# Half of the first product's tiles by seven products over halves of d and of tokens, in blocks 4 to 10 of a retention and Mish feed-forward kernel

## The chip, the cores and the metric

One core of one Trainium2 chip. The metric is the device time of one execution in microseconds (us), the median of several runs. Times inside an execution come from one profiled execution, counted from the start of its span. The engines are TensorE (PE for its matmuls, PEld for its weight loads), VectorE (DVE), ScalarE (ACT), GpSimd (POOL) and SyncE (SP), which issues the DMAs. Each engine takes its instructions in the order in which the program wrote them.

## What is computed

```python
B, H, S, D = 4, 8, 768, 64
state = zeros(B, H, D, D)
for t in range(S):
    state = gamma[h] * state + outer(k[:, :, t], v[:, :, t])
    y[:, :, t] = q[:, :, t] @ state / sqrt(D)
x = y.transpose(0, 2, 1, 3).reshape(3072, 512)
h = x @ w_in                       # 512 x 2048
g = h * tanh(log1p(exp(h)))        # Mish
out = g @ w_out                    # 2048 x 512
```

Inputs and output are float32; the kernel multiplies in float16 and sums in float32.

## The kernel before, in words

**Blocks.** The 3072 tokens are 24 chunks of 128. Block 0 has four chunks, blocks 1 to 10 have two each (256 tokens). The retention is done in chunks: scores and a mask within a chunk, an outer product k v for the state, and the past state for the rest. It yields y in PSUM, which is copied to `xt`, the transposed float16 input of the feed-forward part (128 partitions, 4 parts of d_model, and room for 512 tokens, of which blocks 1 to 10 use the first 256). `w_in` lies in SBUF as eight tiles `wins[s][j]` (128 x 4 parts of d x 256 columns), and `w_out` as four tiles.

**First product.** `g1(blk, u)` (L567) makes two of the sixteen 128-wide tiles of h at a time: for each tile four matmuls (L576) over the four parts of d, with 128x128 weights and 256 tokens as the moving columns, into one PSUM bank; ACT's Mish (L584) turns the bank into `g` in float16. Eight calls make the first product of a block: 64 matmuls and eight Mish operations of 128x512.

**Second product.** `seven(blk, ...)` (L648) computes out = g @ w_out for the 256 tokens by seven products instead of eight, over halves of tokens, of d_ff and of the output's columns. It needs sums of halves of g (`gsums`, made on DVE by `sums_a`, L637 and L638, `sums_b`, L642, and `sums_c`, L646) and sums of halves of w_out (`tmats`, made once, L621 to L624). Each product is eight matmuls of 256 columns (L668). Partial results are copied to SBUF on ACT (`snap`, L674) and added on DVE (`done`, L682); the last one, `done(1, 0)`, is a plain copy (L680).

**What lies between.** In the middle of `seven(blk)` the hook `retain(blk + 1, later)` (L534) issues on PE the past part of y for block blk+1 and, from block 3 on, the scores and outer products of block blk+2 (`ready`, L421 and L428), then the present part (`present_of`, L509); ACT copies y into `xt` (L563). A tiny DVE copy `seen` (L548) orders them. Of what `ready` left in PSUM, `settle(blk)` (L486) makes three states on DVE (L463 or L465, L474, L465), `mask_two(blk)` (L495) masks the scores (L498), and `leave(blk)` (L504) makes the last state (L477, L478), except at the end of a batch. For blocks after 3 (those that are not `tight`, L926) the three are called after the first `g1` of the block ahead (`plan[0]`, L936).

**Queues.** POOL casts the inputs q, k, v of later chunks (L368, L371, L373). In `seven` of blocks 1 and 4 to 7 it begins after `sums_b`, and in those of blocks 2 and 3 after `sums_c`, by way of a tiny POOL copy of `gsums` (`cast_behind`, L920). From block 3 on two chunks are cast in a block, until none is left. SP's queue issues the loads, the stores of the block before, and the DMA that transposes q and k (L379).

**PSUM.** Eight banks: three for the tag "mm", one for "px", and two double banks for "at". `g1` uses "px" for its calls 2 and 5 and "mm" for the others. `seven` uses "px" for four of its products in turn, the last of which `done(1, 0)` reads; the banks are given out in turn, and a new tile waits until the readers of the bank's last tile are done.

Of the kernel before, what the change touches and what calls it, by code (L numbers as in the profile page):

```python
# [9 lines left out]
FP16 = mybir.dt.float16  # L10
FP32 = mybir.dt.float32
AF = mybir.ActivationFunctionType
ALU = mybir.AluOpType
# [3 lines left out]
def kernel(  # L17
# [9 lines left out]
    nc = tc.nc  # L27
    B, H, S, D = q.shape
    d_model, d_ff = moe_w_in.shape
    P = 128  # L30
    C = 128
# [3 lines left out]
    TB = 512  # L35
    CPB = TB // C
    BLOCKS = [4] + [2] * ((NCK - 4) // 2)
    first = [sum(BLOCKS[:i]) for i in range(len(BLOCKS))]
    NFB = d_ff // P
    NBP = d_model // P  # L40
# [3 lines left out]
    scale = float(1.0 / np.sqrt(D))  # L44
    inv_boost3 = float(1.0 / BOOST**3)
# [14 lines left out]
    cpool = ctx.enter_context(tc.tile_pool(name="rn_const", bufs=1))  # L60
# [7 lines left out]
    gp = ctx.enter_context(tc.tile_pool(name="rn_g", bufs=2))  # L68
    op = ctx.enter_context(tc.tile_pool(name="rn_o", bufs=5))
    mmps = ctx.enter_context(  # L70
        tc.tile_pool(name="rn_mmps", bufs=3, space=bass.MemoryType.PSUM))
    pxps = ctx.enter_context(
        tc.tile_pool(name="rn_pxps", bufs=1, space=bass.MemoryType.PSUM))
    atps = ctx.enter_context(
        tc.tile_pool(name="rn_atps", bufs=2, space=bass.MemoryType.PSUM))
# [44 lines left out]
    gtiles, tmats, gsums = {}, [], []  # L120
    ONE = 3
    nload, ncast = [0], [0]
    stores, weight_left = [], []

# [64 lines left out]
    def store_due(now):  # L191
        while stores and stores[0][0] <= now:
            _, dst, osb = stores.pop(0)
            nc.sync.dma_start(dst, osb)
# [291 lines left out]
    def settle(blk):  # L486
        a = first[blk]
        u = held[blk][1]
        for j in range(2):
            us[a + j] = u[:, :, j]  # L490
        mid_of(a)
        state_of(a)
        mid_of(a + 1)

    def mask_two(blk):  # L495
        at = held.pop(blk)[0]
        am = tpp.tile([P, 2, 2, HP, D], FP16, name="am")
        nc.vector.tensor_tensor(  # L498
            am.rearrange("p a j i c -> p (a j i) c"), at.rearrange("p a j i c -> p (a j i) c"),
            tri_half.rearrange("p r c -> p (r c)").unsqueeze(1).broadcast_to((P, 4 * HP, D)), op=ALU.mult)  # L500
        for j in range(2):
            ams[first[blk] + j] = am[:, :, j]

    def leave(blk):  # L504
        state_of(first[blk] + 1)
# [61 lines left out]
    def g1(blk, u):  # L567
        nt = BLOCKS[blk] * C
        per = TB // nt
        aside = u % 4 == 2 if blk == 0 else u in (2, 5)  # L570
        pool, tag = (pxps, "px") if aside else (mmps, "mm")
        h_ps = pool.tile([P, per, nt], FP32, name="h_ps", tag=tag)
        for j in range(per):
            s, f = divmod(u * per + j, FPS)
            for bp in range(NBP):
                nc.tensor.matmul(  # L576
                    h_ps[:, j], wins[s][f // 2][:, bp, f % 2 * P:(f % 2 + 1) * P], xts[blk][:, bp, :nt],
                    start=(bp == 0), stop=(bp == NBP - 1))
        room = NFB * TB // (2 * nt)
        at0, lies = divmod(u * per, room)  # L580
        if lies == 0:
            gtiles[blk, at0] = gp.tile([P, room, nt], FP16, name="g", tag="g", bufs=3)
        gt = gtiles[blk, at0][:, lies:lies + per]
        nc.scalar.activation(gt, h_ps, AF.Mish, scale=inv_boost3)  # L584
        for j in range(per):
            gts[blk, u * per + j] = gt[:, j]
# [47 lines left out]
    def sums_a(blk, half):  # L634
        n = NFB // 4
        (s1, s2, _, _), a11, _, a21, a22 = sum_views(blk, slice(half * n, (half + 1) * n))
        nc.vector.tensor_tensor(s1, a21, a22, op=ALU.add)  # L637
        nc.vector.tensor_tensor(s2, s1, a11, op=ALU.subtract)  # L638
# [5 lines left out]
    def sums_c(blk):  # L644
        (_, s2, _, s4), _, a12, _, _ = sum_views(blk)
        nc.vector.tensor_tensor(s4, a12, s2, op=ALU.subtract)  # L646

    def seven(blk, masks, hooks, last):  # L648
        n, hf = NFB // 2, d_model // 2
        px = pxps.tile([P, hf], FP32, name="o_ps", tag="px")  # L650
        pb = mmps.tile([P, hf], FP32, name="o_ps", tag="mm")
        osb = [op.tile([P, d_model], FP32, name="osb", tag="osb") for _ in range(2)]

        def a(i, j):
            return lambda f: gts[blk, j * n + f][:, i * P:(i + 1) * P]

        def b(i, j):
            return lambda f: wouts[(i * n + f) // FPS][:, f % FPS, j * hf:(j + 1) * hf]

        def s(i):  # L660
            return lambda f: gsums[blk % 2][:, i - 1, f]

        def t(i):
            return lambda f: tmats[(i - 1) // 2][:, (i - 1) % 2, f]

        def mm(o_ps, x, w, first=False):
            for f in range(n):
                nc.tensor.matmul(  # L668
                    o_ps, x(f), w(f), start=first and f == 0, stop=f == n - 1,
                    skip_group_check=True)  # L670

        def snap(o_ps):
            x = op.tile([P, hf], FP32, name="snap", tag="snap", bufs=3)
            nc.scalar.copy(x, o_ps)  # L674
            return x

        def done(i, j, o_ps, plus=None):
            dst = osb[i][:, j * hf:(j + 1) * hf]
            if plus is None:
                nc.vector.tensor_copy(dst, o_ps)  # L680
            else:
                nc.vector.tensor_tensor(dst, o_ps, plus, op=ALU.add)  # L682
            if last:
                nc.sync.dma_start(out_rows(blk, i)[:, j * hf:(j + 1) * hf], dst)

        mm(px, a(0, 0), b(0, 0), True)
        m1 = snap(px)
        mm(pb, a(0, 1), b(1, 0), True)
        done(0, 0, pb, m1)
        sums_b(blk)  # L690
        if blk == 1 or not tight(blk):
            cast_behind(blk, 2)
        for fn, *args in masks:
            fn(*args)
        pe = mmps.tile([P, hf], FP32, name="o_ps", tag="mm")
        if last:
            mm(px, s(2), t(2))
            u2 = snap(px)
        mm(pe, s(1), t(1), True)
        m5 = snap(pe)  # L700
        if not last:
            mm(px, s(2), t(2))
            u2 = snap(px)
        for fn, *args in hooks[0]:
            fn(*args)
        sums_c(blk)
        if blk > 1 and tight(blk):
            cast_behind(blk, 3)
        for fn, *args in hooks[1]:
            fn(*args)  # L710
        mm(px, s(3), t(3))
        done(1, 1, px, m5)
        for fn, *args in hooks[2]:
            fn(*args)
        mm(pe, s(4), b(1, 1))
        done(0, 1, pe, u2)
        mm(px, a(1, 1), t(4))
        done(1, 0, px)
        if not last:
            for i in range(2):  # L720
                stores.append((1 + i, out_rows(blk, i), osb[i]))
# [208 lines left out]
    def plan_of(blk):  # L930
        a = first[blk] + 4
        plan = {u: [] for u in (0, 1, 4, 5, 7)}
        if tight(blk):
            plan[5] = [(get_ready, blk + 1)]
        elif blk + 1 < len(BLOCKS):
            plan[0] = [(settle, blk + 1), (mask_two, blk + 1), (leave, blk + 1)]  # L936
        if blk == 1:
            plan[0] += [(turn_next, a)]
            plan[1] += [(load_to, a + 3)]
        elif blk < ONE:  # L940
            plan[1] += [(next_chunk, a)]
            plan[4] += [(load_to, a + 4)]
        return plan

    first_block()
    for blk in range(1, len(BLOCKS)):
        last = blk + 1 == len(BLOCKS)
        plan = plan_of(blk)
        for u in range(NFB // 2):
            store_due(u)  # L950
            g1(blk, u)
            if u in ((6, 7) if tight(blk) else (5, 7)):
                sums_a(blk, u // 7)
            for fn, *args in plan.get(u, ()):
                fn(*args)
            if weight_left:
                weight_left.pop(0)()
        hooks = [[], [], []]
        if not last:
            later = blk + 2 if ONE <= blk < len(BLOCKS) - 2 else None  # L960
            hooks = [[(retain, blk + 1, later, True)],
                     [(next_two, first[blk] + 6, tight(blk))] if blk >= ONE else
                     [(turn_next, first[blk] + 5), (load_to, first[blk] + 8)] if blk == 1 else
                     [(next_chunk, first[blk] + n) for n in (5, 6, 7)],
                     [(finish, blk + 1)] if later is None else []]
        if tight(blk):
            hooks[2].append((leave, blk + 1))
        seven(blk, [(mask_two, blk + 1)] if tight(blk) else [], hooks, last)
# [31 lines left out]
```

## Time and profile before

| | us |
|---|---|
| median of 3 runs (lowest to highest) | 201.49 (201.34 to 202.06) |
| profiled execution | 201.44 |
| its span, first to last instruction | 199.7 |
| first product of a block, blocks 4 to 10 | 6.99 |
| from one first product's start to the next, blocks 4 to 9 | 14.71, 14.71, 14.71, 14.52, 14.59, 14.31 |
| from block 10's first product to the start of the last DVE copy | 13.29 |
| VectorE busy in those stretches, blocks 4 to 9 | 9.09, 8.62, 7.84, 7.83, 7.82, 7.74 |
| ScalarE busy in them | 7.22, 7.23, 7.22, 7.22, 7.21, 6.62 |
| GpSimd busy in them | 8.43, 6.67, 6.67, 6.48, 2.35, 0.00 |

A line of a timeline gives the start of an instruction, its length, engine, line in the kernel, operation, out<-in with partitions x elements and type, how many were merged, and in brackets the idle time before it with what ended it. The chain of work that ended last is followed back from the last instruction; each of its lines gives a start, a length and what ran. A matmul's own length (0.27 us for 256 columns) contains its way through the array; in a row they start 0.109 us apart. The granted TensorE clock was 1.00 in all stretches.

### The profile page before, as it was taken

To read this page: it belongs to the slowest core of one execution; us is meant where nothing else is said; L and a number is where in the kernel's file an instruction comes from. 1 tells how busy PE (TensorE), PEld (TensorE's weight loads), DVE (VectorE), ACT (ScalarE), POOL (GpSimd) and SP (SyncE) were. 2 spreads that over 40 slices of the span, in tenths; PEclk is the share of its full clock that TensorE was granted. 3 is DMA by queue.
4 is the path that set the end of the run, shared out by engine and by line. 5 is a ranking of instruction groups with operands and counts; after the bars stand their busy time and mean duration, and the time that the engine had idled before them with its cause. 6 is when DMAs were issued, how large, how long until landed. Compare 5 with 4: busy or idle time off the path is not lost.

```text
span 199.7 us, 6553 instructions
## 1 busy us (share of the span) xinstructions
PE 192.4 (96%) x2871; PEld 155.1 (78%) x2871; DVE 111.6 (56%) x204; ACT 92.1 (46%) x166; POOL 74.8 (37%) x93
## 2 busy tenths in 40 slices
PE   7887999999999999999999999999999999999993
PEld 7765444445888888888888888888888888888882
DVE  0688444997359169266836745545753654455052
ACT  2376773242542542554454454454553553642640
POOL 6562000669807603942907508409409300000000
PEclk9999999999999999999999999999999999999999
DMA  5999999999999999999999999996932600201102
GB/s 180 300 316 356 390 382 343 316 254 214 239 232 250 188 214 271 127 215 211 258 155 300 194 232 202 199 225 126 206 121 40 175 3 11 98 3 54 56 26 79
DMA packets 83612, 38.74 MB, mean 194 GB/s; under 512 B 57728, under 2 KB 77696, under 8 KB 83584
## 3 DMA queue, kind: packets, MB, share of 16 engines
q1 hardware_dynamic: 83440, 38.28, 82.0%
q8 instruction: 22, 0.36, 0.8%
q10 hardware_dynamic: 144, 0.05, 0.2%
q14 instruction: 6, 0.05, 0.1%
HBM read 27.31 MB, written 6.29 MB: 168 GB/s over the span
## 4 chain that ended last, share of the span: by engine, by line
PE 69%; DMA 16%; SPq 7%; DVE 3%; POOL 2%; issue 1%; DVEq 0%; POOLq 0%
PE h_ps L576 33%; PE o_ps L668 31%; DMA wi<-in_moe_w_in_dram 5%; DMA wt<-in_moe_w_out_dram 5%; SPq L243 3%; PE y_ps L509 3%; DMA qf<-in_q_dram 3%; DMA qkt<-qk 3%; SPq L160 2%; PE at L421 2%; PE u_ps L428 1%; POOL qk L368 1%; POOL qk L371 1%; DVE win L177 1%; DVE wout L188 1%
## 5 line engine op out<-in xcount | busy, mean ns | idle before, releaser
L576 PE MATMUL h_ps<-xt,win 128*128 128x256 f16 (+1 forms) x704 | 86.0, 282 | 0.8 <-ACT xt L358 0.7
L576 PEld LDWEIGHTS <-win 128*128 128x128 f16 x704 | 68.5, 98 | 16.0 <-POOL win L177 0.9
L584 ACT ACTIVATE g<-h_ps 128x512 f16<-128x512 f32 x96 | 57.3, 597 | 48.3 <-PE h_ps L576 48.3
L668 PEld LDWEIGHTS <-gsum 128*128 128x128 f16 x320 | 30.1, 98 | 4.5 <-DVE gsum L646 0.7
L668 PE MATMUL o_ps<-tmat,gsum 128*128 128x256 f16 x240 | 29.4, 273 | 0.0
L668 PEld LDWEIGHTS <-g 128*128 128x128 f16 x240 | 23.5, 98 | 2.7
L637 DVE TENSOR_TENSOR gsum<-g 128x512 f16<-128x512 f16 x20 | 8.6, 429 | 28.4 <-ACT g L584 28.4
L674 ACT COPY snap<-o_ps 128x256 f32<-128x256 f32 x30 | 11.2, 372 | 21.5 <-PE o_ps L668 21.5
L368 POOL TENSOR_TENSOR qk<-qf,qvs 128x512 f16<-128x512 f32 x18 | 19.5, 1086 | 3.6 <-DMA qf<-in_q_dram 2.5
L373 POOL TENSOR_TENSOR v<-vf,qvs 128x512 f16<-128x512 f32 x18 | 20.7, 1148 | 0.0
L923 POOL COPY summed<-gsum 128x1 f16<-128x1 f16 x7 | 1.3, 187 | 51.7 <-DVE gsum L642 36.9
L371 POOL TENSOR_TENSOR qk<-kf,qvs 128x512 f16<-128x512 f32 x18 | 20.1, 1118 | 0.0
L682 DVE TENSOR_TENSOR osb<-o_ps,snap 128x256 f32<-128x256 f32 x30 | 12.7, 424 | 12.4 <-PE o_ps L668 7.4
L668 PE MATMUL o_ps<-wout,g 128*128 128x256 f16 x160 | 19.1, 273 | 0.0
L563 ACT CAST xt<-y_ps 128x512 f16<-128x512 f32 x15 | 10.2, 733 | 11.3 <-PE y_ps L509 11.3
L590 PE MATMUL o_ps<-wout,g 128*128 128x512 f16 x64 | 15.0, 380 | 0.0
L465 DVE TENSOR_TENSOR mid<-u_ps,sth 128x256 f16<-128x256 f32 x15 | 6.3, 422 | 10.1 <-PE u_ps L428 9.8
L498 DVE TENSOR_TENSOR am<-at,tri_half 128x1024 f16<-128x1024 f32 x9 | 10.9, 1216 | 0.0
L590 PEld LDWEIGHTS <-g 128*128 128x128 f16 x64 | 5.8, 97 | 6.6
L668 PE MATMUL o_ps<-wout,gsum 128*128 128x256 f16 x80 | 10.4, 274 | 0.0
L668 PE MATMUL o_ps<-tmat,g 128*128 128x256 f16 x80 | 10.4, 273 | 0.0
L392 PE MATMUL at<-ident 128*128 128x128 f16 (+1 forms) x79 | 8.0, 276 | 1.4 <-POOL ident L96 1.4
(77 smaller groups left out, 184.0 us busy)
## 6 DMA issues: line engine op xcount, KB each, us to landing
kf<-in_k_dram SPq DMA_DIRECT2D x24, 256.0 KB, 4.8
vf<-in_v_dram SPq DMA_DIRECT2D x24, 256.0 KB, 5.3
out_dram<-osb SPq DMA_DIRECT2D x22, 256.0 KB, 3.9
qf<-in_q_dram SPq DMA_DIRECT2D x20, 256.0 KB, 4.1
wt<-in_moe_w_out_dram SPq DMA_DIRECT2D x3, 1024.0 KB, 9.8
wi<-in_moe_w_in_dram SPq DMA_DIRECT2D x4, 512.0 KB, 8.5
wi<-in_moe_w_in_dram SPq DMA_DIRECT2D x2, 1024.0 KB, 10.6
qfirst<-in_q_dram SPq DMA_DIRECT2D x2, 512.0 KB, 4.6
```

What stands on the lines that cost most here:

```text
L368: nc.gpsimd.tensor_tensor(q16.rearrange("p (r h) d -> p h r d", r=2), qf, qs_two[:, heads].unsqueeze(3).broadcast_to((P, H // 2, 2, D)), o ...
L371: nc.gpsimd.tensor_tensor(k16, kf, boosts.unsqueeze(2).broadcast_to((P, H, D)), op=ALU.mult)
L373: nc.gpsimd.tensor_tensor(v16, vf, vs[g % 2].unsqueeze(2).broadcast_to((P, H, D)), op=ALU.mult)
L498: nc.vector.tensor_tensor(am.rearrange("p a j i c -> p (a j i) c"), at.rearrange("p a j i c -> p (a j i) c"), tri_half.rearrange("p r c -> ...
L563: nc.scalar.copy(dst[:, :, :, s], src)
L576: nc.tensor.matmul(h_ps[:, j], wins[s][f // 2][:, bp, f % 2 * P:(f % 2 + 1) * P], xts[blk][:, bp, :nt], start=(bp == 0), stop=(bp == NBP - 1))
L584: nc.scalar.activation(gt, h_ps, AF.Mish, scale=inv_boost3)
L590: nc.tensor.matmul(o_ps, gts[blk, fb][:, t * P:(t + 1) * P], wouts[s][:, f, cols], start=(fb == 0), stop=(fb == NFB - 1))
L637: nc.vector.tensor_tensor(s1, a21, a22, op=ALU.add)
L668: nc.tensor.matmul(o_ps, x(f), w(f), start=first and f == 0, stop=f == n - 1, skip_group_check=True)
L674: nc.scalar.copy(x, o_ps)
L682: nc.vector.tensor_tensor(dst, o_ps, plus, op=ALU.add)
```

## The change

In blocks 4 to 10 the eight calls of `g1` are replaced by `mixed_in(blk, last)`.

- Tiles 4 to 7 and 12 to 15 of h are made as before, two at a time (`plain`).
- Tiles 0 to 3 and 8 to 11 are made by seven products of halves: halves of d_model, of the 256 tokens, and the two groups of four tiles. Each product (`mm`) is four tiles times two parts of d, that is eight matmuls with 128x128 weights and 128 tokens as moving columns, into one bank of 128x512. Three intermediate results go to SBUF by ACT copies (`kept`: m1, m5, u2), three sums are made on DVE from PSUM and SBUF (`plus`: h11, h12, h22), and Mish reads those from SBUF; the fourth quarter is read from PSUM.
- The sums of halves of `w_in` (`in_sums`) are made once on DVE: four operations of 128x512 each in block 2 and in block 3, one behind each of the first `g1` calls.
- The sums of halves of x (`x_sums`) are four DVE operations of 128x256 each, into the unused columns of `xt`. They are issued in `seven(blk)` for block blk+1, between `done(0, 1)` and the last product with `done(1, 0)`, for blk 3 to 9.
- `settle`, `mask_two` and `leave` for the next block move: `settle` ahead of the first of the products, `mask_two` behind the second, `leave` behind the sixth, ahead of `sums_a` for the first half.
- The banks: pp, pf, pa and the second plain pair take "mm" in this order; pm and the third plain pair take "px", the last plain pair takes "at".

```diff
+    def in_sums(j):
+        t = cpool.tile([P, 4, 2, TB // 2], FP16, name=f"wsum_{j}")
+        wsums.append(t)
+        (a11, a12), (a21, a22) = [(x[:, :2], x[:, 2:]) for x in (wins[0][j], wins[2][j])]
+        sub = ALU.subtract
+        return [
+            lambda: nc.vector.tensor_tensor(t[:, 0], a21, a22, op=ALU.add),
+            lambda: nc.vector.tensor_tensor(t[:, 1], t[:, 0], a11, op=sub),
+            lambda: nc.vector.tensor_tensor(t[:, 2], a11, a21, op=sub),
+            lambda: nc.vector.tensor_tensor(t[:, 3], a12, t[:, 1], op=sub),
+        ]
+
+    def x_views(blk):
+        xt = xts[blk]
+        b = [[xt[:, 2 * i:2 * i + 2, j * C:(j + 1) * C] for j in range(2)] for i in range(2)]
+        t = [xt[:, i, 2 * C:].rearrange("p (k c) -> p k c", k=2) for i in range(4)]
+        return b, t
+
+    def x_sums(blk):
+        ((b11, b12), (b21, b22)), t = x_views(blk)
+        for to, a, b in ((t[0], b12, b11), (t[1], b22, t[0]), (t[2], b22, b12), (t[3], b21, t[1])):
+            nc.vector.tensor_tensor(to, a, b, op=ALU.subtract)
+
+    def mixed_in(blk, last):
...
+        def mm(o_ps, w, x, begin=False):
+            for f in range(n):
+                for k in range(2):
+                    nc.tensor.matmul(
+                        o_ps[:, f], w(f // 2, k)[:, f % 2 * P:(f % 2 + 1) * P], x[:, k],
+                        start=begin and f == 0 and k == 0, stop=k == 1, skip_group_check=True)
...
+        def mish(to, src):
+            nc.scalar.activation(to, src, AF.Mish, scale=inv_boost3)
...
+        def kept(o_ps):
+            m = op.tile([P, n, C], FP32, name="hsum", tag="hsum", bufs=6)
+            nc.scalar.copy(m, o_ps)
+            return m
+
+        def plus(x, y):
+            m = op.tile([P, n, C], FP32, name="hsum", tag="hsum", bufs=6)
+            nc.vector.tensor_tensor(m, x, y, op=ALU.add)
+            return m
+
+        pp = bank(mmps, "mm", True)
+        pf = bank(mmps, "mm")
+        pa = bank(mmps, "mm")
+        if not last:
+            settle(blk + 1)
+        mm(pa, a(0, 0), b[0][0], True)
+        m1 = kept(pa)
+        mm(pf, s(1), t[0], True)
+        m5 = kept(pf)
+        if not last:
+            mask_two(blk + 1)
+        plain(pp, n)()
+        pm = bank(pxps, "px")
+        mm(pm, a(0, 1), b[1][0], True)
+        h11 = plus(pm, m1)
+        mm(pa, s(2), t[1])
+        u2 = kept(pa)
+        mish(part(0, 0), h11)
+        mm(pf, s(4), b[1][1])
+        h12 = plus(pf, u2)
+        mish(part(0, 1), h12)
+        plain(bank(mmps, "mm", True), n + 2)()
+        mm(pa, s(3), t[2])
+        h22 = plus(pa, m5)
+        mish(part(1, 1), h22)
+        if not last:
+            leave(blk + 1)
+        sums_a(blk, 0)
+        plain(bank(pxps, "px", True), 3 * n)()
+        mm(pa, a(1, 1), t[3])
+        mish(part(1, 0), pa)
+        ph = atps.tile([P, 2, 2, 2 * C], FP32, name="h_ps", tag="at")[:, 0]
+        plain(ph, 3 * n + 2)()
+        sums_a(blk, 1)
 
     def seven(blk, masks, hooks, last):
...
         mm(pe, s(4), b(1, 1))
         done(0, 1, pe, u2)
+        if not last and blk >= ONE:
+            x_sums(blk + 1)
         mm(px, a(1, 1), t(4))
         done(1, 0, px)
...
-        elif blk + 1 < len(BLOCKS):
-            plan[0] = [(settle, blk + 1), (mask_two, blk + 1), (leave, blk + 1)]
...
+        if blk > ONE:
+            mixed_in(blk, last)
+        elif blk > 1:
+            weight_left.extend(in_sums(blk - 2))
         for u in range(NFB // 2):
             store_due(u)
+            if blk > ONE:
+                continue
             g1(blk, u)
```

More of the change, by code (lines that the diff above doesn't have):

```diff
@@ L122 @@
     nload, ncast = [0], [0]
-    stores, weight_left = [], []
+    stores, weight_left, wsums = [], [], []
     def room(g):
@@ new lines, in x_views, with a, s, part @@
+    def x_views(blk):
[8 more added lines that the diff above has]
+    def mixed_in(blk, last):
+        b, t = x_views(blk)
+        n = NFB // 4
+        gt = gtiles[blk, 0] = gp.tile([P, NFB, 2 * C], FP16, name="g", tag="g", bufs=3)
+        for f in range(NFB):
+            gts[blk, f] = gt[:, f]
+        def mm(o_ps, w, x, begin=False):
[4 more added lines that the diff above has]
+                        start=begin and f == 0 and k == 0, stop=k == 1, skip_group_check=True)
+        def a(i, j):
+            return lambda h, k: wins[2 * i][h][:, 2 * j + k]
+        def s(i):
+            return lambda h, k: wsums[h][:, i - 1, k]
+        def mish(to, src):
+            nc.scalar.activation(to, src, AF.Mish, scale=inv_boost3)
+        def part(i, j):
+            return gt[:, i * 2 * n:i * 2 * n + n, j * C:(j + 1) * C]
+        def plain(h_ps, f0):
+            for f in range(2):
+                w, h = divmod(f0 + f, n)
+                for k in range(NBP):
+                    nc.tensor.matmul(
+                        h_ps[:, f], wins[w][h // 2][:, k, h % 2 * P:(h % 2 + 1) * P],
+                        xts[blk][:, k, :2 * C], start=k == 0, stop=k == NBP - 1)
+            return lambda: mish(gt[:, f0:f0 + 2], h_ps)
+        def bank(pool, tag, whole=False):
+            return pool.tile([P, 2, 2 * C] if whole else [P, n, C], FP32, name="h_ps", tag=tag)
+        def kept(o_ps):
[40 more added lines that the diff above has]
+        sums_a(blk, 1)
```

## The prediction

> **What bounds the kernel now.** First the page's busy times, then the chain of work that ended last, then the timelines of VectorE (DVE) and GpSimd (POOL) where one block ends and the next begins.
>
> ```profile
> PE 192.4 (96%) x2871; PEld 155.1 (78%) x2871; DVE 111.6 (56%) x204; ACT 92.1 (46%) x166; POOL 74.8 (37%) x93
> ```
>
> TensorE (PE) is busy for 96% of the span. The chain, printed as start, length, what, says that in blocks 4 to 10 it is the bound by itself; one block's start:
>
> ```profile
> 110.57 6.99 PE h_ps L576 x64
> 117.56 3.49 PE o_ps L668 x32
> ```
>
> The first product's 64 matmuls take 6.99 us, 109 ns each, in every one of the seven blocks, with no wait in them; the period of a block is 14.71 us in blocks 4 to 6, then 14.52, 14.59 and 14.31. A PE saving would thus count in full, if nobody comes late. DVE at such a boundary (start, length, line; blocks 5 to 6, whose first product begins at 125.12, called T0 below):
>
> ```profile
> 124.52 0.42 DVE L682 TENSOR_TENSOR osb<-o_ps,snap 128x256 f32<-128x256 f32 x1 [0.59 <-PE o_ps L668]
> 125.32 0.42 DVE L680 COPY osb<-o_ps 128x256 f32<-128x256 f32 x1 [0.38 <-PE o_ps L668]
> 125.66 0.41 DVE L465 TENSOR_TENSOR mid<-u_ps,sth 128x256 f16<-128x256 f32 x1
> 126.11 0.42 DVE L474 TENSOR_TENSOR sth<-u_ps,mid 128x256 f16<-128x256 f32 x1
> 126.57 0.42 DVE L465 TENSOR_TENSOR mid<-u_ps,sth 128x256 f16<-128x256 f32 x1
> 126.91 1.21 DVE L498 TENSOR_TENSOR am<-at,tri_half 128x1024 f16<-128x1024 f32 x1
> ```
>
> DVE works through this without a gap, and nobody waits for it, since the next sums are due only at T0+6. POOL is casting in the same stretch:
>
> ```profile
> 121.71 1.04 POOL L371 TENSOR_TENSOR qk<-kf,qvs 128x512 f16<-128x512 f32 x1
> 122.71 1.49 POOL L373 TENSOR_TENSOR v<-vf,qvs 128x512 f16<-128x512 f32 x1
> 124.17 1.05 POOL L368 TENSOR_TENSOR qk<-qf,qvs 128x512 f16<-128x512 f32 x1
> 125.19 1.03 POOL L371 TENSOR_TENSOR qk<-kf,qvs 128x512 f16<-128x512 f32 x1
> 126.19 1.03 POOL L373 TENSOR_TENSOR v<-vf,qvs 128x512 f16<-128x512 f32 x1
> ```
>
> And DVE's sum s4, two f16 inputs in SBUF, beside them:
>
> ```profile
> 121.83 1.47 DVE L646 TENSOR_TENSOR gsum<-g,gsum 128x1024 f16<-128x1024 f16 x1
> ```
>
> Alone that shape takes 0.68 (L646 at 165.74). Here it ends at 123.30, so it worked from 122.62, 0.13 before the POOL record at 121.71 ends; and the next POOL operation took 1.49 for 1.04. The two engines exclude each other. Two such sums in a row lose to POOL each time:
>
> ```profile
> 35.70 1.55 DVE L621 TENSOR_TENSOR tmat<-wout 128x1024 f16<-128x1024 f16 x1
> 37.28 1.43 DVE L622 TENSOR_TENSOR tmat<-wout,tmat 128x1024 f16<-128x1024 f16 x1
> ```
>
> Sums that read PSUM (L465, L682) keep their 0.42 beside POOL.
>
> **The change, part by part.** *PE.* 32 matmuls of 256 columns (32 x 0.109 = 3.49 us) become 56 of 128 columns. No steady stretch of before has these in a first product; nearest are the transposes, 128 columns with new weights each:
>
> ```profile
> 6.21 0.62 PE L215 MATMUL t_ps<-ident,qk 128*128 128x128 f16 x8
> 6.21 0.45 PEld L215 LDWEIGHTS <-qk 128*128 128x128 f16 x8
> ```
>
> (0.62 - 0.22) / 7 = 57 ns, the 0.22 being one matmul's own length. The ends are 50 ns (the weight loads' spacing, (0.45 - 0.10) / 7) and 98 ns (a load's own length); I take 56.5. A product is then 0.45 us, seven 3.16, and the stage 6.65 against 6.99: 0.34 less per block, 2.4 us in seven blocks, if PE never waits.
>
> *Operations added, per block.* ACT copies m1, m5, u2 (128x512, PSUM): L219's 0.58; ends 0.37 (256 wide, L674) and 0.73 (L563). DVE adds h11, h12, h22 (128x512, PSUM plus SBUF): between 0.42 (256 wide, L682) and 1.22 (1024 wide, L498), on that line 0.69, and L602's copy of that size has 0.68; I take 0.69. DVE's x_sums, four of 128x256 f16: L637 (512 wide) 0.42 and L646 (1024) 0.68 give 0.295; ends 0.16 (the one-column copy) and 0.42; I take 0.30. Mish is as often and as wide as before; half of it reads SBUF (L256 there: 0.63 for 0.60). Back to back, ACT operations start 0.1 and DVE's 0.07 before the one ahead ends.
>
> *DVE's queue.* x_sums stands between L682 (ends T0-0.18) and L680, which frees the bank px; behind L680 wait settle (L465, L474, L465), mask_two (L498), and only then h11, h12, h22. POOL's L368 ends at T0+0.10, L371 and L373 follow at once. So t0 works from -0.03 to 0.27; L371 then ends at 1.17, t1 works 1.04 to 1.34; L373 ends at 2.24, t2 works 2.11 to 2.41; POOL is done, t3 ends at 2.64. The four, 1.1 us alone, take 2.8. L680 then starts at 2.57 and ends at 2.99; by the spacings above settle starts 0.34 later, mask_two another 1.25, h11 another 1.13: h11 from 5.29 to 5.98, h12 to 6.60, h22 to 7.22.
>
> *PE against it* (0.06 from a DVE end to PE). M1, M5 and the first plain pair end at 1.78. The next product needs px: 3.05, a wait of 1.27, with all of PE's later work queued behind it. It, two more products, a plain pair and another product end at 5.73. The plain pair in px needs h11: 6.04 (wait 0.31), ends 6.91. The last product needs h22's read: 7.28 (wait 0.37), and the last pair ends at 8.61. ACT starts the first mixed mish at 6.03 and has six in a row: the one that frees px ends at 8.72, so the second product starts at 8.78 instead of 6.99: **+1.79 per block**. ACT's last ends at 9.70; its values are used at about 10.4, and sums_a ends at 10.6 where the second product's first add on DVE is due at 10.8. So the rest keeps its length.
>
> *By blocks.* 5, 6, 7: 3 x 1.79 = 5.37. Block 8: POOL's L368 ends 0.25 later against T0 (154.70): 2.04. Block 4: four POOL operations (95.51 to 99.57) lie behind L682, and which engine is first at 95.5 is open: 1.6 to 3.4, I take 2.5. Blocks 9, 10: POOL is through at 156.7, x_sums ends by T0+0.9. In 9, h22 ends at 5.47 and PE and ACT lose 0.35 again: 0.0. Block 10 has no settle or mask: PE waits only 0.07, -0.27.
>
> *in_sums*, four sums of 0.42 in blocks 2 and 3: in block 2 DVE has been idle for 4.98 us before L465 (70.82), which hides them. In block 3 (idle 4.78) POOL casts from 80.08 to 87.34; the four end at about 85.4, just ahead of L465 at 85.84, but push POOL by some 1.2 us, and with it the transposing DMA issued at 86.58, whose 4.7 us to landing ended near the use at 92: 0 to 0.8, I take 0.4. No path below nothing: they free nothing.
>
> settle, mask_two and leave come later but their readers (past_of, ready) stand 10 us on. The stores keep their order in SP's queue; POOL's queue still starts from sums_b.
>
> Sum: 2.5 + 5.37 + 2.04 + 0.0 - 0.27 + 0.4 = **+10.0 us**. The profiled execution took 201.44 (span 199.7, 1.7 around it; the median of the runs is 201.49): **211.5 us**.
>
> **Rivals.** *A, DVE keeps the way free* and x_sums runs in 1.1 us beside POOL as well. For: t1 to t3 follow closely. Against: L622. Then blocks 4 to 8 go like 9: 0.0 each, so -0.27 + 0.4: 201.6, no change.
>
> *B, the PE saving comes through.* Place: DVE's queue before h22. It decides at L680 starting by T0+0.6 (h22 ends 4.65 after it, PE gets there at 5.3), with the mish in px done in time. Then -2.4 us: 199.0. For: block 10 nearly does it. Against: even without POOL, L680 starts at 0.8; with it, at 2.6.
>
> *C, weight loads pace the small matmuls.* At 98 ns a product takes 0.78 and the stage at least 7 x 0.78 + 3.49 = 8.98, so blocks 9 and 10 lose 2.0 each. In blocks 5 to 7 the third product still starts at 3.05, and what follows it (five products at 0.78, three pairs at 0.87) ends at 9.6 without a wait: +2.6 each; block 8 +2.85, block 4 +3.3, block 3 +0.4; in all +18.3: 219.8. For: PEld's 98 ns is longer than 57. Against: the transposes, eight in a row.
> The Trainium skill ("TensorE: Matmul & The Clock Gate", Back-to-back issue gap) puts a steady stream of load and matmul with 128 columns at about 81 ns each. By it a product would take 0.65 and the time come to about 214.8, my estimate from that page; the transposes here, at 57, don't show it, though they are only eight at a time.
>
> **Numbers.** Forecast 0.78, A 0.09, B 0.08, C 0.05. The forecast's own bounds: if t1 and t2 pass in one POOL gap, 0.9 less in each of five blocks, and block 3 and 4 at their low ends: 205.5; if x_sums' operations take 0.42 (+0.25 a block), ACT gives no overlap (+0.4 a block) and blocks 3 and 4 stand at their high ends: 217. The range 205.5 to 217 holds the forecast and C's lower half, about 8 in 10. A run of this kernel can tell about 0.5% (1.0 us) from no change: faster 0.08 (B), same 0.09 (A), slower 0.83.
>
> **What would show it.** x_sums' rows: with POOL busy, about 0.5 to 1.1 each in blocks 5 to 8, 0.30 in 9 and 10. PE idle before the third product of blocks 4 to 8 with DVE's L680 named. The first stage 8.6 us in blocks 5 to 7 and about 7 in block 9. Products at 0.45 us, else C. If the stage is 6.65 throughout, or x_sums rows are all 0.3, the forecast is wrong; also if the second product grows, for I cost it at nothing.

## The result, and the profile after

The changed kernel takes 211.25 us against 201.49: a ratio of 1.0474 (95% interval 1.0444 to 1.0503), slower. Of its four runs three took 210.95 to 211.44 us; the fourth, in a slow state, took 388.21 us, counts in the median and not in the ratio. The prediction was 211.5 us, range 205.5 to 217. The profiled execution took 211.44 us, 10.0 us more than that of before; its span is 209.5 us, 9.87 us more.

In the listing after the change L682 is a small product, L702 a plain pair, L669 x_sums, L717 the adds h11, h12, h22; old L668, L680 and L682 are now L775, L787 and L789, and old L584 stands as L693 in the mixed blocks. The busy times of the page:

```profile
PE 194.0 (93%) x3039; PEld 155.4 (74%) x3039; DVE 148.5 (71%) x261; ACT 100.4 (48%) x187; POOL 76.4 (36%) x93
```

TensorE's share of the span fell from 96 to 93%: it now waits. The chain of work that ended last, over the stage that before read "110.57 6.99 PE h_ps L576 x64" and nothing else (here block 6, first product from 130.13 to 138.79):

```profile
129.95 0.44 DVE xt L669
...
130.41 2.27 DVE xt L669 x3
132.68 0.35 DVE osb L787
...
133.07 1.07 PE h_ps L682 x16
...
134.18 0.45 DVE am L498
...
135.31 0.69 DVE hsum L717
...
136.03 2.73 ACT g L693 x5
```

It no longer lies on TensorE: it runs through x_sums, the copy that frees px, mask_two, the adds and the Mish operations behind them. The timelines of DVE, of POOL and then of PE in that stretch:

```profile
129.52 0.42 DVE L789 TENSOR_TENSOR osb<-o_ps,snap 128x256 f32<-128x256 f32 x1 [0.59 <-PE o_ps L775]
129.87 2.81 DVE L669 TENSOR_TENSOR xt<-xt 128x256 f16<-128x256 f16 x4
132.60 0.41 DVE L787 COPY osb<-o_ps 128x256 f32<-128x256 f32 x1
...
134.18 1.21 DVE L498 TENSOR_TENSOR am<-at,tri_half 128x1024 f16<-128x1024 f32 x1
135.31 1.88 DVE L717 TENSOR_TENSOR hsum<-h_ps,hsum 128x512 f32<-128x512 f32 x3
```

```profile
129.18 1.05 POOL L368 TENSOR_TENSOR qk<-qf,qvs 128x512 f16<-128x512 f32 x1
130.19 1.08 POOL L371 TENSOR_TENSOR qk<-kf,qvs 128x512 f16<-128x512 f32 x1
131.24 1.09 POOL L373 TENSOR_TENSOR v<-vf,qvs 128x512 f16<-128x512 f32 x1
```

```profile
130.13 0.61 PE L682 MATMUL h_ps<-xt,win 128*128 128x128 f16 x8
130.57 0.61 PE L682 MATMUL h_ps<-xt,wsum 128*128 128x128 f16 x8
131.02 1.04 PE L702 MATMUL h_ps<-xt,win 128*128 128x256 f16 x8
133.07 0.61 PE L682 MATMUL h_ps<-xt,win 128*128 128x128 f16 x8 [1.01 <-DVE osb L787]
133.51 1.06 PE L682 MATMUL h_ps<-xt,wsum 128*128 128x128 f16 x16
134.41 1.04 PE L702 MATMUL h_ps<-xt,win 128*128 128x256 f16 x8
135.28 0.61 PE L682 MATMUL h_ps<-xt,wsum 128*128 128x128 f16 x8
136.04 1.03 PE L702 MATMUL h_ps<-xt,win 128*128 128x256 f16 x8 [0.15 <-DVE hsum L717]
137.24 0.61 PE L682 MATMUL h_ps<-xt,win 128*128 128x128 f16 x8 [0.16 <-DVE hsum L717]
```

Four sums take 2.81 us beside the casts; one by one they take 0.51, 1.02, 1.13 and 0.28 us, and the first three end about 0.15 us behind the end of one of the three casts. The view of the line L669 has the shortest, the median and the longest of all 28 sums, in ns:

```profile
L669 DVE TENSOR_TENSOR xt<-xt x28: 277/514/1142, 96.5 to 193.9; 128x256 f16<-128x256 f16 x28
```

The matmuls that should start at 131.9 (131.02 and eight times 0.109) start at 133.07, and two more waits follow. The products themselves start 0.44 to 0.45 us apart.

The table has the time from one first product's start to the next (for block 10, to the last DVE copy), read from TensorE's timelines:

| block | 3 | 4 | 5 | 6 | 7 | 8 | 9 | 10 |
|---|---|---|---|---|---|---|---|---|
| before | 15.67 | 14.71 | 14.71 | 14.71 | 14.52 | 14.59 | 14.31 | 13.29 |
| after | 16.34 | 17.01 | 16.39 | 16.38 | 16.22 | 16.49 | 14.19 | 13.00 |
| difference | +0.67 | +2.30 | +1.68 | +1.67 | +1.70 | +1.90 | -0.12 | -0.29 |

With 0.36 us that lie ahead of block 2, where no changed instruction has run yet (block 2 starts at 64.95 before and 65.31 here, and between 64.99 and 65.94 in the other runs), the differences add to 9.87 us, the whole of it. In each of blocks 4 to 8 the growth is in the first product: the rest of block 6, from the second product's start to the next block, takes 7.7 us in both kernels.

### The profile page after: what moved, and what is told of

The parts are those of the page before. It is cut to its first block, busy times and chain, and to the rows that moved or that the text cites. A ratio compares the mean times of both kernels' runs of the same rounds, so it can differ in the third digit from the quotient of the medians.

```text
span 209.5 us, 6998 instructions
## 1 busy us (share of the span) xinstructions
PE 194.0 (93%) x3039; PEld 155.4 (74%) x3039; DVE 148.5 (71%) x261; ACT 100.4 (48%) x187; POOL 76.4 (36%) x93
## 4 chain that ended last, share of the span: by engine, by line
PE 44%; DMA 18%; DVE 13%; ACT 7%; SPq 6%; POOL 6%; issue 4%; DVEq 0%; POOLq 0%
PE o_ps L775 26%; DVE xt L669 7%; ACT g L693 7%; PE h_ps L682 6%; DMA qkt<-qk 5%; DMA wi<-in_moe_w_in_dram 5%; DMA wt<-in_moe_w_out_dram 5%; PE h_ps L576 4%; DMA qf<-in_q_dram 3%; PE h_ps L702 3%; SPq L243 3%; PE y_ps L509 3%; POOL qk L371 3%; SPq L160 2%; POOL qk L368 2%
## 5 line engine op out<-in xcount | busy, mean ns | idle before, releaser
L576 PE MATMUL h_ps<-xt,win 128*128 128x256 f16 (+1 forms) x256 | 36.0, 299 | 0.8 <-ACT xt L358 0.7
L775 PEld LDWEIGHTS <-gsum 128*128 128x128 f16 x320 | 30.0, 98 | 4.6 <-DVE gsum L646 0.7
L584 ACT ACTIVATE g<-h_ps 128x512 f16<-128x512 f32 x40 | 23.9, 597 | 19.1 <-PE h_ps L576 19.1
L576 PEld LDWEIGHTS <-win 128*128 128x128 f16 x256 | 24.6, 98 | 11.0 <-POOL win L177 0.9
L702 PE MATMUL h_ps<-xt,win 128*128 128x256 f16 x224 | 29.0, 273 | 0.8 <-DVE hsum L717 0.8
L775 PE MATMUL o_ps<-tmat,gsum 128*128 128x256 f16 x240 | 29.4, 273 | 0.0
L775 PEld LDWEIGHTS <-g 128*128 128x128 f16 x240 | 23.4, 97 | 4.1 <-issue 1.4
L702 PEld LDWEIGHTS <-win 128*128 128x128 f16 x224 | 20.9, 97 | 3.4 <-issue 1.4
L712 ACT COPY hsum<-h_ps 128x512 f32<-128x512 f32 x21 | 11.7, 587 | 22.2 <-PE h_ps L682 22.2
L789 DVE TENSOR_TENSOR osb<-o_ps,snap 128x256 f32<-128x256 f32 x30 | 12.7, 424 | 11.5 <-PE o_ps L775 6.5
L693 ACT ACTIVATE g<-h_ps 128x512 f16<-128x512 f32 x35 | 19.2, 592 | 1.4 <-PE h_ps L702 1.4
L775 PE MATMUL o_ps<-wout,g 128*128 128x256 f16 x160 | 19.1, 272 | 0.4
L682 PE MATMUL h_ps<-xt,win 128*128 128x128 f16 x168 | 12.8, 219 | 6.6 <-DVE osb L787 5.8
L682 PEld LDWEIGHTS <-win 128*128 128x128 f16 x168 | 11.1, 97 | 8.9 <-issue 8.4
L669 DVE TENSOR_TENSOR xt<-xt 128x256 f16<-128x256 f16 x28 | 16.7, 636 | 0.2
L693 ACT ACTIVATE g<-hsum 128x512 f16<-128x512 f32 x21 | 13.0, 627 | 7.0 <-DVE hsum L717 7.0
L637 DVE TENSOR_TENSOR gsum<-g 128x512 f16<-128x512 f16 x20 | 9.3, 465 | 9.8 <-ACT g L693 8.1
```

Source lines behind the costliest of these rows:

```text
L576: nc.tensor.matmul(h_ps[:, j], wins[s][f // 2][:, bp, f % 2 * P:(f % 2 + 1) * P], xts[blk][:, bp, :nt], start=(bp == 0), stop=(bp == NBP - 1))
L669: nc.vector.tensor_tensor(to, a, b, op=ALU.subtract)
L682: nc.tensor.matmul(o_ps[:, f], w(f // 2, k)[:, f % 2 * P:(f % 2 + 1) * P], x[:, k], start=begin and f == 0 and k == 0, stop=k == 1, skip_g ...
L693: nc.scalar.activation(to, src, AF.Mish, scale=inv_boost3)
L702: nc.tensor.matmul(h_ps[:, f], wins[w][h // 2][:, k, h % 2 * P:(h % 2 + 1) * P], xts[blk][:, k, :2 * C], start=k == 0, stop=k == NBP - 1)
L712: nc.scalar.copy(m, o_ps)
```

## The experiments

Two theories stand behind a loss of this form: that VectorE's sums and GpSimd's casts exclude each other (the prediction's), or that VectorE's queue is simply too long. Each result is compared with runs of the kernel before on the same chip.

**The casts moved away from the sums**

```diff
         if not last and blk >= ONE:
             x_sums(blk + 1)
+            cast_second(blk)
...
+    def cast_second(blk):
+        g = first[blk] + 7
+        if g < NCK:
+            nc.gpsimd.tensor_copy(summed, xts[blk + 1][:, 3, TB - 1:])
+            turn_next(g)
```

(`cast_behind` casts one chunk less, and `next_two` leaves the second chunk's transposing DMA to `turn_next`.)

> The changed kernel with GpSimd's second chunk of casts in blocks 3 to 7 held back until the four sums of x are done (and its transposing DMA with it), so that the sums on VectorE meet no cast. Nothing is left out. Theory (VectorE and GpSimd exclude each other, and the sums stand ahead of the copy that frees px): the sums take about 1.0 us in blocks 5 to 8 as they now do in 9 and 10, and the periods of blocks 4 to 8, now 2.30, 1.68, 1.67, 1.70 and 1.90 us over those of before, fall to block 9's (0.1 under before): about 201.5 us, up to 202.5 if block 4's first sums still meet a cast. Rival L (VectorE's queue is too long with the sums, the three adds, settle and mask_two, whoever else runs): blocks 4 to 8 keep at least 1 us each, 206 us or more. Rival P (128-column products are paced by their weight loads): no change, 211.

Measured: 203.25 us against 201.55, ratio 1.0096 (1.0067 to 1.0125). That is above the 202.5 that I allowed; still, about 8 of the nearly 10 us are gone by moving GpSimd's casts, and the DMA behind them, alone. DVE's timeline, same place as above, and the casts that now follow the sums:

```profile
125.52 0.42 DVE L789 TENSOR_TENSOR osb<-o_ps,snap 128x256 f32<-128x256 f32 x1 [0.58 <-PE o_ps L775]
125.86 1.01 DVE L669 TENSOR_TENSOR xt<-xt 128x256 f16<-128x256 f16 x4
126.79 0.41 DVE L787 COPY osb<-o_ps 128x256 f32<-128x256 f32 x1
```

```profile
127.00 0.19 POOL L1035 COPY summed<-xt 128x1 f16<-128x1 f16 x1 [1.79 <-DVE xt L669]
127.14 1.06 POOL L368 TENSOR_TENSOR qk<-qf,qvs 128x512 f16<-128x512 f32 x1
```

The same four sums take 1.01 instead of 2.81 us. Blocks 5, 7 and 8 need 14.62, 14.40 and 14.45 us, each about 0.1 under before, as forecast. The rest that was not expected: block 4, 15.31 (one of its four sums still met a cast, which the expectation allowed), block 3, 15.97 (the sums of w_in, below), and block 6, 15.55, with a wait of TensorE of 0.95 us in the second product that the profile puts down to nothing useful (an unnamed wait; the last section comes back to these). The theory of a long queue, 206 or more, falls.

**The sums moved to GpSimd**

```diff
-            nc.vector.tensor_tensor(to, a, b, op=ALU.subtract)
+            nc.gpsimd.tensor_tensor(to, a, b, op=ALU.subtract)
```

(and GpSimd's second chunk of casts stands behind them)

> The changed kernel with the four sums of x on GpSimd, between its two chunks of casts, so that VectorE does none of them. Nothing is left out. Theory: the copy that frees px starts 0.2 us after the first product's begin as before, TensorE hardly waits in the first stage (about 6.7 us against 6.99), and the seven blocks gain 0.2 to 0.3 us each; with the 1.0 us that was lost ahead of block 4: about 200.5 us (200 to 201.5). Rival L: part of the loss stays, since the three adds, settle and mask_two remain on VectorE: 203 or more. Rival G (GpSimd is too slow for the sums, over 0.8 us each, so that the second product waits for them): above 203, with TensorE waiting for GpSimd ahead of the second and fourth of the small products.

Measured: 203.25 us against 201.55, ratio 1.0097 (1.0063 to 1.0132): a miss in size. The stage behaved as expected, 6.70 to 6.71 us in blocks 5 to 10, and blocks 7, 8 and 9 need 14.36, 14.30 and 14.03, about 0.2 to 0.3 under before. But block 4 took 16.44 us, 1.73 more than before. POOL and PE there, and the chain:

```profile
97.81 2.67 POOL L669 TENSOR_TENSOR xt<-xt 128x256 f16<-128x256 f16 x4
```

```profile
98.52 0.61 PE L682 MATMUL h_ps<-xt,wsum 128*128 128x128 f16 x8 [0.92 <-POOL xt L669]
```

```profile
104.98 4.75 DMA qkt<-qk
```

The sums stand behind three casts in GpSimd's queue, so the second product waits 0.92 us for the first of them; in this block that is the wait of rival G, though a sum takes 0.67 us and not over 0.8. The sums then pushed the casts of the last chunk, and its transposed q and k came 0.87 us after TensorE wanted them. That part is a loss of the same kind as in block 3, by way of GpSimd's queue and SP's. Block 6 took 15.06 us, with an unnamed wait of 0.58.

**No sums of x at all**

```diff
-        t = [xt[:, i, 2 * C:].rearrange("p (k c) -> p k c", k=2) for i in range(4)]
+        t = [b[0][1], b[1][1], b[0][1], b[1][0]]
...
-            x_sums(blk + 1)
```

> The changed kernel without the sums of x: the products that should read them read unsummed halves of x instead, as many and as large, so the first product's mixed half is a different value. The casts stay where they are. Theory: as with the sums on another engine, 200.5 us (200 to 201.2), the stage 6.7 us: what the rest of the change (three adds, three copies, seven small products, moved settle and mask_two, sums of weights) costs and saves by itself. Rival L: 203 or more. Rival P: 207 or more.

Measured: 202.34 us, from 200.26 to 203.41 in ten runs, against 201.55; ratio 1.0015 (0.9984 to 1.0046): above the 200 to 201.2 that I expected. The profile is of the longest of the ten runs. The stage is 6.69 or 6.70 us in six of the seven blocks, so three adds, three copies and the moved settle and mask_two cost TensorE nothing. The gain is about 0.3 us per block, and waits that the profile doesn't name took it back in this execution: block 5 needed 15.90 us, block 6 15.02. In block 5:

```profile
113.24 0.62 PE L682 MATMUL h_ps<-xt,wsum 128*128 128x128 f16 x8 [0.93 <-issue]
```

The time agrees with the theory only to within these waits; it lies under the 203 of a long queue.

**The sums of x alone, in the kernel before**

```diff
         done(0, 1, pe, u2)
+        if not last and blk >= ONE:
+            x_sums(blk + 1)
         mm(px, a(1, 1), t(4))
```

> The kernel before with only the four sums of x added where the change has them; nobody reads them. Theory: the copy that frees px ends about 3.0 us into the first product in blocks 5 to 8, where the third call of the plain first product needs px at 1.75 us: about 1.3 us more per block in blocks 4 to 8, none in 9 and 10: 208 us (207 to 209.5). Rival L (the sums hurt only together with the adds): 201.5 to 203.

Measured: 208.5 us against 201.55, ratio 1.0345 (1.033 to 1.036), as expected. Nobody reads these sums; they cost 7 us by their place. DVE and PE of block 6 (T0 128.27; in this listing L657 is x_sums and L691 the copy that frees px):

```profile
128.01 2.81 DVE L657 TENSOR_TENSOR xt<-xt 128x256 f16<-128x256 f16 x4
```

```profile
128.27 1.91 PE L576 MATMUL h_ps<-xt,win 128*128 128x256 f16 x16
131.21 5.40 PE L576 MATMUL h_ps<-xt,win 128*128 128x256 f16 x48 [1.03 <-DVE osb L691]
```

The third call of the plain first product waits for px, freed by the copy behind the sums. Blocks 4 to 8 lose 1.82, 1.18, 1.18, 1.20 and 1.42 us, blocks 9 and 10, where GpSimd has no casts, none. The changed kernel loses 0.5 us more in each of blocks 4 to 8: its adds stand further down the same queue, and its timeline of TensorE above has two more waits, both for them.

**px freed ahead of the sums**

```diff
-        if not last and blk >= ONE:
-            x_sums(blk + 1)
         mm(px, a(1, 1), t(4))
         done(1, 0, px)
+        if not last and blk >= ONE:
+            x_sums(blk + 1)
```

> The changed kernel with the four sums of x behind the copy that frees px instead of ahead of it, so that TensorE's longest wait in the profile, the one for px, goes. Nothing is left out. Theory (the length of VectorE's queue up to the last add sets the stage, with the sums stretched by the casts; px is only the first place where it shows): the second product then waits 0.9 us for the first sum, the adds still start about 5.1 us into the stage, and the time hardly moves: 210.0 to 211.2. Rival W (the wait for px is the cost): each of blocks 4 to 8 gains about 1 us, 205 to 207.

Measured: 212.12 us against 201.80, ratio 1.0524 (1.0504 to 1.0543). Removing the longest wait in the profile gained nothing. PE, block 5 (T0 114.25):

```profile
115.56 0.61 PE L682 MATMUL h_ps<-xt,wsum 128*128 128x128 f16 x8 [0.70 <-DVE xt L669]
...
119.99 1.03 PE L702 MATMUL h_ps<-xt,win 128*128 128x256 f16 x8 [0.29 <-DVE hsum L717]
121.19 0.61 PE L682 MATMUL h_ps<-xt,win 128*128 128x128 f16 x8 [0.16 <-DVE hsum L717]
```

The wait moved to the second product, which needs the first sum, and the adds set the end as before: blocks 5 to 8 take 16.21, 16.20, 16.10 and 16.25 us, 0.1 to 0.2 less than in the changed kernel. That the whole came out above my 211.2 lies in blocks 4, 9 and 10 (17.66, 14.66 and a stage of 7.14 us), which I had left out of the expectation. In 9 and 10 the second product now waits 0.27 us for a sum. In block 4 it waits 0.44, all four sums meet casts (3.62 us from 97.13), and TensorE waits 2.01 us for the first add.

**The sums of w_in alone, in the kernel before** (`in_sums` and its call added, nobody reads them)

> The kernel before with only the eight sums of w_in added in blocks 2 and 3, where the change has them; nobody reads them. Theory: they hold up GpSimd's casts in block 3 by about 1 us, the transposed q and k come late, and block 3's period grows by 0.5 to 0.8 us: 202.0 to 202.5 us. Rival: they lie in VectorE's idle time and cost nothing, 201.5, and block 3's loss in the changed kernel came from something else.

Measured: 202.15 us against 201.80, ratio 1.0023 (1.0009 to 1.0037), about 0.5 us with an interval from 0.2 to 0.75. Block 3 needs 15.98 instead of 15.67. So they are not free for that block, though VectorE is idle there: GpSimd's casts wait for them (four of them take 1.22 to 1.24 us instead of 1.04 to 1.05), and the transposed q and k come late. Block 4 then needs 14.52 instead of 14.71, so in this execution 0.1 us of the loss is left; the rest of its longer span, 0.5 us, lies ahead of block 2, where no sum has run.

**Mending both: sums on GpSimd, all sums of w_in in block 2, casts earlier in block 3**

```diff
-        elif blk > 1:
-            weight_left.extend(in_sums(blk - 2))
+        elif blk == 2:
+            weight_left.extend(in_sums(0) + in_sums(1))
...
-        if blk == 1 or not tight(blk):
+        if blk != 2:
             cast_behind(blk, 2)
-        if blk > 1 and tight(blk):
+        if blk == 2:
             cast_behind(blk, 3)
...
```

> The run with the sums of x on GpSimd, and two more edits: all eight sums of w_in are made in block 2 (two behind each call), so that GpSimd's casts in block 3 meet no sum; and in block 3 GpSimd begins its casts behind sums_b instead of sums_c, so that the sums of x for block 4 and its transposed q and k come 2.5 us earlier. Nothing is left out. Theory: with the sums off VectorE the first stages take 6.70 us (6.98 before), and the rest of the loss of that run was q and k arriving late in blocks 3 and 4: blocks 3 and 4 are back to before's 15.7 and 14.7, seven stages give 2.0 us, so 199.5 to 200.5 us. Rival (the rest is noise of the run or instruction supply, not q and k): above 201.5, with the profile's nameless waits in place of the DMA.

Measured: 201.98 us against 201.80, ratio 1.0008 (0.9985 to 1.003): no difference from before, and a miss. Block 3 is back to 15.67 and block 4 to 14.67 (q and k are 0.24 us late by way of SP's queue); blocks 7 to 9 need 14.36, 14.31 and 14.02. Block 5 took 15.28 and block 6, 15.41, with unnamed waits of 0.75 and 0.93 us. The view names GpSimd's sums for the first of them, but TensorE starts that product at 111.84, and the sum that it reads ended at 110.08. So what is left is the rival of this expectation.

**SP's transposing DMA ahead of three loads, on top of that**

```diff
             turn_next(first[blk] + 7)
+            load_to(first[blk] + 10)
...
         turn_next(g)
-        load_to(g + 4)
```

> The last version (sums of x on GpSimd, sums of w_in all in block 2, casts in block 3 from sums_b on) with one more edit: in blocks 3 to 9 SP issues the second chunk's transposing DMA ahead of three of the loads instead of behind them. Nothing is left out. Theory: in the last version blocks 4 and 5 lost about 0.3 and 0.9 us because q and k of block 6 came 1.8 us late behind those loads, and then the sums of x; with that gone, 1 us less than that version, 200.3 to 201.2 us, 0.3 to 0.7% under before. Rival (what is left is not the SP queue but waits that the profile doesn't name): no change, 202.

Measured: 202.57 us against 202.19, ratio 1.0022 (1.0 to 1.0045): a miss. Blocks 4 and 5 did come down, to 14.35 and 14.70 (in block 5 with an unnamed wait of 0.17 us in place of 0.75), but blocks 6 and 7 took 15.36 and 15.46. PE in block 6's second product:

```profile
137.04 1.05 PE L775 MATMUL o_ps<-tmat,gsum 128*128 128x256 f16 x8
138.97 1.05 PE L775 MATMUL o_ps<-wout,gsum 128*128 128x256 f16 x8 [0.88 <-DVE osb L789]
```

The lower of them reads s4, done at 137.97 (L646, 136.51 and 1.46), and in the kernel before it starts 0.06 us after it. The view names a DVE operation that has nothing for it, and the chain has 0.35 us there as "issue". Block 7 has another such wait, of 1.15 us. So the rival of that expectation, waits that the profile doesn't name, holds for what is left.

**Small matmuls alone, in the kernel before**

```diff
+            step = C if blk > ONE and u % 4 < 2 else nt
+            for c in range(0, nt, step):
+                for bp in range(NBP):
...
```

> The kernel before, in which calls 0, 1, 4 and 5 of the first product in blocks 4 to 10 are made by matmuls of 128 tokens instead of 256: 32 large and 64 small ones, each with its own weight load. Nothing else differs and nothing is left out. Theory (a small matmul with new weights starts every 56.5 ns, as the changed kernel's products do): the stage is 7.1 us instead of 6.98, 0.1 per block and 0.8 us in all, a ratio of 1.004 to before. Rival P (weight loads pace them when they come 16 in a row): at 81 to 98 ns the stage is 8.7 to 9.8 us, 12 us or more in all. Rival I (TensorE's instructions come too late when there are more of them in the same time, which would be the nameless waits of the faster versions): nameless waits of about 1 us in some of blocks 5 to 7, a ratio of 1.009 or more.

Measured: 203.12 us against 201.98, ratio 1.0053 (1.0034 to 1.0072). The stage is 7.06 to 7.08 us: with 3.49 for the 32 large ones, 64 small ones take (7.07 - 3.49) / 64 = 56 ns each, and weight loads don't pace them. Block 5 took 15.90 us, where blocks 4 and 6 took 14.88 and 14.78. It has an unnamed wait at the product that reads s4, as in block 6 above:

```profile
124.93 1.05 PE L670 MATMUL o_ps<-wout,gsum 128*128 128x256 f16 x8 [1.05 <-DVE osb L684]
```

This kernel differs from before by nothing but the number of matmuls in the first products, so these waits come with more instructions on TensorE in the same time. That the instructions themselves arrive late is what the traces of all these runs show together (last section).

## Why the prediction was right, step by step

- **What bounds the kernel.** Right: TensorE's saving counts where nobody comes late. Where GpSimd was silent it did, of 0.3 us a part in block 9 and all in block 10 (-0.12 and -0.29; forecast 0.0 and -0.27).
- **A product's price.** 56.5 ns a matmul forecast, 56 measured. The Trainium skill ("TensorE: Matmul & The Clock Gate", Back-to-back issue gap) has about 81 ns for such a stream; neither the products here nor the 64 small matmuls a block of the last experiment show it.
- **The operations added.** Adds 0.69 forecast, 0.68 measured (L717); ACT copies 0.58 and 0.59 (L712); a sum of x alone 0.30 and 0.28; Mish from SBUF 0.63 and 0.63. The straight line through two sizes of the same operation was good to 0.02 us.
- **VectorE against GpSimd.** Four sums beside the casts: 2.8 us forecast, 2.81 measured. Moving the casts (1.01) and the sums alone in the kernel before (2.81 and 7 us in the time) show this as the cause, not only as a reading of the profile. The Trainium skill ("SBUF — State Buffer", Who interferes with whom) states that a VectorE instruction with two SBUF inputs contends with a GpSimd instruction that reads SBUF, and that the ports which the two share are an exclusive lock; these runs agree, and show the price for short operations in a row: a sum of 0.28 us took up to 1.14.
- **The path to the end of the stage.** Forecast against block 6, from T0: px free 2.99 and 2.88; third product 3.05 and 2.94; first add from 5.29 and 5.18; last add ends 7.22 and 7.06; second product 8.78 and 8.66. It ran 0.1 to 0.16 us early; by the forecast's own chain a sum of 0.28 in place of 0.30 us accounts for 0.08 of that.
- **By blocks.** 1.79 forecast for 5 to 7, 1.67 to 1.70 measured; block 8, 2.04 and 1.90; block 4, 2.5 and 2.30. Block 4's figure was the middle of an open choice, 1.6 to 3.4, so that it came near is luck. The second product, costed at nothing, kept its 7.7 us.
- **The weak term** was in_sums: 0.4 us forecast with a bound of 0.8; block 3 grew by 0.67 in the changed kernel, and 0.3 in the run with the sums alone. The way was right (GpSimd's casts, then the DMA). The 0.36 us ahead of block 2 was in no term; since it lies before the first changed instruction and differs between the runs, I count it to none. The terms together (10.0) are 0.5 us above what blocks 3 to 10 grew by (9.51); that the whole time was met to 0.25 us is in part luck.
- **The rivals.** A (the sums run freely beside GpSimd) is the state that moving the casts makes, and there blocks 5, 7 and 8 are within 0.15 us of A's price. C falls by the 56 ns. B, the saving in full, was reached in stages of 6.70 us when the sums left VectorE, but never in the whole time: besides late q and k it met a limit that the forecast had no term for, TensorE's wait for its own instructions, about 1 us in one to three blocks (last section).

## What to carry to other kernels

Before work is added to an engine that looks half idle, look at which instructions stand behind it in that engine's queue, when they are due, and what another engine does at that moment: here 1.0 us of sums in the wrong 3 us cost 7. A run of short VectorE operations with both inputs in SBUF is placed where GpSimd is silent, or GpSimd's work is held until it is through, which needs one small copy. That took away most of the loss here; no version was faster than the kernel before. And removing the longest wait of a profile gains only what the next one on the same queue leaves: follow the queue to its last due instruction, as the run with px freed first shows. A saving on the bounding engine that comes with more and smaller instructions can be lost to the supply of these instructions.

## What the runs showed of the hardware that was not expected

TensorE can wait about 1 us for the next piece of its own program, and the views give that wait no name, or a wrong one. There are nine unnamed waits of 0.54 to 1.15 us in the traces: one in block 6 of each of the five versions whose casts were moved or whose sums left VectorE, one in block 5 of two of these (the run without sums of x and the one that mends both), one in block 7 of a third (the run with the transposing DMA ahead of loads), and one in block 5 of the kernel before with 96 instead of 64 matmuls in its first product, all with a granted clock of 0.998 or more.

The traces show two things that the nine have in common. The first is their place. Counted from the start, 3262, 3774, 4286 or 4798 of TensorE's weight loads and matmuls stand ahead of each of them. These numbers are 512 apart, and they hold whatever block and product come there: the second product of block 5, the product that reads s4 in block 5 or 6, or another one in block 7. The second is a transfer. Each wait ends 1.4 to 1.7 us after a transfer of 16 KB has landed in the DMA queue that the page calls "instruction", here of the kernel before and of the changed one:

```profile
q8 instruction: 22, 0.36, 0.8%
q8 instruction: 23, 0.38, 0.8%
```

The 22 transfers stand beside 5742 weight loads and matmuls, one for about 260. In the kernel before the last transfer has landed 3.5 to 7.6 us before TensorE comes to the first three of these places, and TensorE doesn't wait there. In the slower changed kernel it has landed about 1.5 us or more before, and no unnamed wait over 0.1 us is left. So the unnamed waits are TensorE's instructions coming late. No run moves these transfers alone, and why they start so late is not shown.
